# Ordering a planned kernel by due times counted back from the layers' matmuls

## The chip, the cores and the metric

One Trainium2 chip, of which the kernel uses one core. The time is that of one execution on the device, in microseconds (us); lower is better. The engines are TensorE (PE, its weight loads shown apart as PEld), VectorE (DVE), ScalarE (ACT), GpSimd (POOL) and SyncE (SP, which here issues every DMA). Each engine works through its own instructions strictly in the order in which they stand in the program, so an instruction that waits holds up all that stand behind it on its engine.

## What is computed

Eight batches of eight heads, 576 tokens, 64 values per head. Attention is computed twice: on tokens averaged in fours (144 of them), and locally, each token with the three before and the three after it. The sum of both goes through a maxout layer (three products with 512x768 weights, elementwise maximum) and an output layer of 768x512.

```python
def _attn_ref(q, k, v):
    ...
    q_d = q.reshape(B, H, Sd, factor, D).mean(axis=3)      # factor 4; k_d, v_d alike
    out_d = sm_attn(q_d, k_d, v_d)
    out_up = np.repeat(out_d, factor, axis=2)
    mask = np.abs(pos[:, None] - pos[None, :]) < factor
    scores = np.where(mask, scale * np.matmul(q, k.transpose(0, 1, 3, 2)), -1000000000.0)
    ...
    return (out_up + np.matmul(attn, v)).astype(np.float32)

def _moe_ref(x, w1, w2, w3, w_out):
    h = np.maximum(np.maximum(x @ w1, x @ w2), x @ w3)
    return (h @ w_out).astype(np.float32)
```

## The kernel before

**The work.** The 4608 tokens are nine blocks of 512 (`j` = 0 to 8; block 8 holds the last 64 tokens of every batch). Each half block of four heads has a number `n` = 2j or 2j+1. A block is first attended to, then its 512 columns go through the layers.

**The layers.** Every fp32 operand is split into a high and a low part (`hi`, `lo`) of a type that TensorE takes in one pass, and a product is three matmuls of 128x512: hi by hi, lo by hi, hi by lo. `mlp_column(j, ft, tag)` makes one of six columns of the maxout layer: three groups of 12 matmuls, each into a PSUM bank of the four called `pm`, with ACT and DVE taking the bank out (`t`, then the maximum, then `h` and its low part). `mlp_out(j)` is the output layer, four groups of 18. By the loops there are 2556 matmuls of 128x512; below they are called layer matmuls. Blocks 7 and 8 go through most of the layers together (`joint_in`), with seven products in place of eight.

**The attention.** For blocks 0 and 1 (`dense(j)`) local attention is matmuls: `band_scores` multiplies q by k in a band, `band_values` transposes the probabilities on PE (tiles `pst`, `pstb`), copies them from PSUM (`ptb`, in the buffer `y`), multiplies by v (`pxb`, bank `pq`) and copies that out (`xb`, buffer `x`). The averaged attention of the same half block (`tail_pooled`, `pooled_scores`, `band_pooled_values`, `pooled_values`) ends in `od`. `transposes(j, c)` adds both to `xs` and splits it into `xhi`, `xlo`, which the layers read. For blocks 2 to 8 (`block(j)`, `attention(n)`) local attention is elementwise: DVE multiplies (`prod`) and sums (`sums`), POOL or ACT multiplies by v (`pv`), DVE or POOL sums that (`x`).

**The weights.** 24 pieces of 512 KB (18 of the maxout layer, six of the output layer) arrive as pairs of 32-bit words and are turned into fp32 in `weight_split`: on DVE four operations on a buffer `wa` (its name in the trace is `hqk`) and a subtraction that makes `wlo` or `wo`, on ACT an absolute value and a cast.

**What sets the order.** Nothing is issued as the code runs. A `Recorder` takes each operation with the engines that could do it (`forms`), and `place()` then plays the engines by a table of prices (`price`): at each turn it takes, among the operations whose inputs are there, the one with the smallest key, puts it on the engine that ends first, and `emit()` writes the program in the order so found. Before the change the key is the time at which the operation could start, then `prio` (a number given where the operation is recorded: half blocks by 100.0 * n, matmuls 2000 lower), then the place in the code. Constants put margins into it: `LAG`, `LAG0`, `MLP`, `PE_LAG`, `BANK_LAG` (how long after its inputs an operation counts as ready) and `SPARE` (how much later than another engine DVE may be and still be chosen). PE's price is multiplied by `COLD` between `WARM` and `SLOW`.

```python
key = (t if t > now + PATIENCE[e] else now, o.prio, o.seq)
...
if e == "PE" and WARM < t < SLOW:
    c *= COLD
```

Every instruction of the trace has one line of the source, L459 (`emit`), so the rows are told apart by tiles.

Of the kernel before, what the change touches and what calls it, by code (L numbers as in the profile page):

```python
# [21 lines left out]
P = 128  # L22
# [10 lines left out]
QS = 1.0 / 128.0  # L33
QB = 1.0 / 8.0
XBUFS = 5
LAG = 678.77
LAG0 = 117.1
MLP = 601.0
PE_LAG = 2038.91
BANK_LAG = 1596.4  # L40
SEG = FAC * P
NDENSE = 2
FIRST = (0.0, 4.72, 44.91, 49.39)
LATE = (1.3, 0.0, 0.4, 9.0)
WPRIO = (20.0, 60.0, 105.0, 150.0, 160.0, 170.0, 180.0)
# [32 lines left out]

ENGINES = ("PE", "DVE", "ACT", "POOL", "SP")
DONE_NS = {"PE": 230.0, "DVE": 150.0, "ACT": 190.0, "POOL": 200.0}  # L80
SPARE = 1649.2
PATIENCE = {"PE": 0.0, "DVE": 142.18, "ACT": 0.0, "POOL": 0.0, "SP": 0.0}
LANES = 8
RING = 128
DMA_FIRST = 1300.0
DMA_LAST = 1100.0
SLOW = 82000.0
SWITCH = {("R", "P"): 120.0, ("P", "R"): 110.0, ("P", "T"): 25.0, ("T", "P"): 93.0, ("t", "P"): 90.0, ("P", "t"): 90.0, ("B", "P"): 96.0, ("M", "P"): 100.0, ("P", "M"): 20.0, ("R", "T"): 10.0, ("T", "R"): 5.0, ("R", "M"): 91.0, ("T", "M"): 93.0, ("M", "R"): 300.0, ("M", "T"): 305.0, ("M", "B"): 0.0, ("B", "M"): 96.0, ("B", "R"): 120.0, ("t", "R"): 90.0, ("R", "t"): 95.0, ("t", "M"): 90.0, ("t", "B"): 90.0, ("t", "T"): 90.0, ("T", "t"): 90.0, ("M", "t"): 100.0}
COLD = 1.65
WARM = 11000.0  # L90


def is_ap(a):
# [19 lines left out]
    return "P" if kind == "M" and elems(args[0]) in (P, 6) else kind  # L113


class Rings:
    def __init__(self):
        self.free = [0.0] * 16
# [4 lines left out]
    def issue(self, t, on_chip, outside):  # L123
        src, dst = [[list(d) for d in ap.ap] for ap in (outside, on_chip)]
        run = src.pop()[1] if src[-1][0] == 1 and len(src) > 1 else 1
        rows = int(np.prod([c for _, c in src]))
        k = max(x for x in range(1, 17) if src[0][1] % x == 0 and dst[0][1] % x == 0)
        each = rows // k
        lane = self.count % LANES
        self.count += 1  # L130
        t = max(t, self.lanes[lane])
        while True:
            left = sum(n * min(1.0, (b - max(t, a)) / (b - a)) for a, b, n in self.queue if b > t)
            if left + each <= RING or not left:
# [4 lines left out]
        work = each * (8.5 + 0.0377 * 4 * run) * (1.25 if rows > P and run > P else 1.0)  # L139
        for e in range(k):  # L140
            begin = max(self.free[e], t + DMA_FIRST)
            self.free[e] = begin + work
            if e == 0:
                self.queue.append((begin, begin + work, each))
        end = max(self.free[:k]) + DMA_LAST
        self.lanes[lane] = end
        return t, done, end


class Recorder:  # L150
# [93 lines left out]
    def price(self, eng, method, args, kw):  # L244
# [7 lines left out]
        if eng == "PE":  # L252
            rows, cols = list(args[1].ap)[0][1], elems(args[1])
            if method == "transpose":
                return (109.0 if rows == P and cols in (D, P) else 185.0 if rows > 32 else 29.0), False
            if args[1].dtype == F32R:
                return 228.5, False
            if args[1].dtype == BF16:
                return 125.0, False
            if n == SD:  # L260
                return 14.0 if cols == T32 else 66.0 if rows == T32 else 135.0 if rows == P else 209.0, False
            if cols <= D and (rows <= 16 or cols <= T32):
                return 57.0, False
            return 165.0 if n > P else 125.0, False
        if eng == "DVE":
            if method == "memset":
                return 60.0 + 0.3 * n, False
# [20 lines left out]
    def place(self):  # L288
# [45 lines left out]
        while len(out) < len(ops):  # L334
            best = None
            for e in ENGINES:
                if not queue[e]:
                    continue
                now = free[e]
                pick = None  # L340
                for o in queue[e]:
                    t = max(now, o.ready)
                    if o.cost[e][1]:
                        t = max(t, port)
                    key = (t if t > now + PATIENCE[e] else now, o.prio, o.seq)
# [19 lines left out]
            if e == "PE":  # L365
                kind = pe_kind(o)
                c += SWITCH.get((last_kind, kind), 0.0)
                last_kind = kind
            if e == "PE" and WARM < t < SLOW:
                c *= COLD  # L370
            o.eng, o.start = e, t
            if e == "SP":
                ap = next(a for a in (o.forms[e][0][1][:2]) if a.tensor.name in self.of)
# [31 lines left out]
                wake(tag)  # L405
        self.out = out
        return out

    def stuck(self, ops):
        done = set(map(id, self.out))  # L410
# [60 lines left out]
def local_global_attention_maxout_kernel(ctx: ExitStack, tc: tile.TileContext, q, k, v, qt_dense, kt_dense, qt_pool, kt_pool, qkt_tail, v_dense, v_tail, w_in, w_out, ident_d, mask_d, band_d, out):  # L471
# [51 lines left out]
    state = {"pieces": 0, "wo": []}  # L523


    def row_tokens(t, j, h, tok, n, p0=0, p1=P):
# [107 lines left out]
    def pooled_scores(n):  # L634
# [15 lines left out]
        for i in range(2):  # L650
            dve.tensor_reduce(out=nm[:, 2 * i : 2 * i + 2], in_=sps[i], axis=AX.X, op=ALU.max, negate=True)
        dve.tensor_reduce(out=nm[:, 4:5], in_=spt, axis=AX.X, op=ALU.max, negate=True)
        dve.tensor_scalar_mul(nm, nm, QS)
        for x in range(4):
            i, pr = x // 2, x % 2
            act.activation(sps[i][:, pr], sps[i][:, pr], AF.Exp, bias=nm[:, x : x + 1], scale=QS, accum_out=zd[:, x : x + 1])
# [9 lines left out]
        dve.tensor_scalar_mul(dt[:, TAIL:], spt[:, P:], rd[:, 4:5])  # L666
        rec.add(forms)
        dve.transpose(ptt[:, :T32], dt)
        for i in range(2):
# [143 lines left out]
    def band_scores(n, pr, tag):  # L813
# [7 lines left out]
        for tp in range(2):  # L821
# [13 lines left out]
            dve.tensor_scalar_mul(mx[:, :, 2 * tp : 2 * tp + 2], mx[:, :, 2 * tp : 2 * tp + 2], QB)  # L835
            for i in range(2):
                for u in range(2):
                    x = 2 * tp + u
# [293 lines left out]
    def dense(j):  # L1132
# [20 lines left out]
        if j == 0:  # L1153
            order = [load[a][0], load[b][0], load[a][1], load[b][1]] + scores[a] + sums[a] + values[a] + scores[b] + sums[b] + values[b] + [(a, pooled, 0), (b, pooled, 0)]
        else:
            order = load[a] + scores[a] + sums[a] + values[a] + load[b]
            order += [scores[b][0], sums[b][0], (a, pooled, 0), values[b][0], scores[b][1], sums[b][1], values[b][1], (b, pooled, 0)]
        for x in order:
            step(*x)

    def block(j):
        rec.spare = SPARE
# [9 lines left out]

    def weights(f, *which):
        for x in which:
            with at(40.59 + state["pieces"] * 1.14):
                f(x)

    with at(-2.0):
        load_constants()
# [69 lines left out]
```

## Time and profile before

| | |
|---|---|
| time, three runs | median 741.54 us (740.58 to 741.93) |
| the profiled execution, span from first to last instruction | 742.2 us |
| PE busy | 712.6 us, 96% of the span |
| DVE busy | 658.4 us, 89% |
| ACT busy | 422.8 us, 57% |
| POOL busy | 331.9 us, 45% |
| read from and written to HBM | 82.0 and 9.4 MB |

The profiled execution has no time of its own beside its span; the span lies 0.7 us over the median of the runs. PE's busy time counts a matmul from its start to a modelled end, and these overlap: a layer matmul counts 0.39 us and the next starts 0.23 us after it. So a PE that is 96% busy isn't 96% at work, and the clock that the profile shows as granted (PEclk, 1.00 is 2.4 GHz and 0.50 is 1.2 GHz) has to be read beside it.

### The profile page before, as it was taken

What the parts mean: (1) busy time and instruction counts of PE and PEld (TensorE: products, weight loads), DVE (VectorE), ACT (ScalarE), POOL (GpSimd) and SP (SyncE); (2) the same over time, 40 slices, a digit from 0 to 9 for tenths busy, and PEclk for the clock granted to TensorE, in tenths of its full rate; (3) what the DMA queues carried; (4) which work ended last, traced back from release to release, by engine and by line L of the source; (5) the groups of instructions that cost most, each with busy time, mean ns of one, the idle gap of its engine ahead of it and who ended that gap; (6) DMA issues with size and microseconds to landing.
All of it is one profiled execution on the core that took longest, in us unless ns stands there. A gap on an engine that the chain in (4) does not pass through costs nothing.

```text
span 742.2 us, 11812 instructions
## 1 busy us (share of the span) xinstructions
PE 712.6 (96%) x3820; PEld 566.6 (76%) x3820; DVE 658.4 (89%) x980; ACT 422.8 (57%) x1415; POOL 331.9 (45%) x545
## 2 busy tenths in 40 slices
PE   5877899999999999999999999999999999999996
PEld 3654677878788778777887787878778888888885
DVE  6999998999999998999999999999989999988520
ACT  4776767526484557557473748577395547433221
POOL 0001001038894739585573858788186336321000
PEclk9769999999999999999999999999999999999999
DMA  8954334265555535653454444633342310000012
GB/s 265 332 198 146 93 93 150 89 186 193 167 168 164 154 92 153 185 165 108 150 160 139 127 140 149 181 97 122 93 136 77 105 47 28 1 1 0 1 57 57
DMA packets 51561, 92.20 MB, mean 124 GB/s; under 512 B 5645, under 2 KB 21311, under 8 KB 51499
## 3 DMA queue, kind: packets, MB, share of 16 engines
q1 hardware_dynamic: 51498, 91.45, 39.3%
q8 instruction: 30, 0.49, 0.3%
q14 instruction: 33, 0.26, 0.1%
HBM read 81.99 MB, written 9.44 MB: 123 GB/s over the span
## 4 chain that ended last, share of the span: by engine, by line
PE 84%; DVE 7%; DMA 6%; SPq 1%; issue 1%; ACT 0%; ACTq 0%; DVEq 0%
PE pm L459 71%; PE pa L459 13%; DVE hqk L459 3%; DMA whi<-in_kt_dense_dram 2%; DMA pv<-in_kt_dense_dram 1%; DMA wo<-in_w_in_dram 1%; DMA hh<-in_w_in_dram 1%; DVE wlo_0r L459 1%; PE pq L459 1%; DMA v<-in_v_dram 1%; SPq L459 1%; DMA pv<-in_moe_w_out_dram 1%; DVE t L459 0%; DVE mxb L459 0%; DVE xlo_0r L459 0%
## 5 line engine op out<-in xcount | busy, mean ns | idle before, releaser
L459 PE MATMUL pm<-xhi_0r,whi_0r 128*128 128x512 f32 x552 | 218.3, 395 | 0.0
L459 PE MATMUL pm<-xhi_0r,wlo_0r 128*128 128x512 f32 x552 | 218.2, 395 | 0.0
L459 PE MATMUL pm<-xlo_0r,whi_0r 128*128 128x512 f32 x552 | 216.7, 397 | 0.0
L459 POOL TENSOR_TENSOR pv<-v,sums 128x256 f32<-128x256 f32 x244 | 146.7, 703 | 15.8 <-DMA v<-in_v_dram 6.0
L459 ACT ACTIVATE pv<-v,sums 128x64 f32<-128x64 f32 x536 | 141.5, 414 | 13.9 <-POOL sums L459 6.4
L459 PE MATMUL pm<-wo_0r,hh_0r 128*128 128x512 f32 x576 | 138.3, 393 | 0.5 <-DVE wo_0r L459 0.5
L459 PEld LDWEIGHTS pm<-wo_0r,hh_0r 128*128 128x128 f32 x576 | 106.7, 188 | 23.2 <-DVE wo_0r L459 0.9
L459 PEld LDWEIGHTS pm<-xlo_0r,whi_0r 128*128 128x128 f32 x552 | 103.9, 189 | 23.2 <-issue 1.1
L459 PEld LDWEIGHTS pm<-xhi_0r,wlo_0r 128*128 128x128 f32 x552 | 104.3, 189 | 22.6 <-issue 1.5
L459 PEld LDWEIGHTS pm<-xhi_0r,whi_0r 128*128 128x128 f32 x552 | 104.2, 189 | 21.8 <-issue 0.7
L459 DVE TENSOR_REDUCE sums<-prod 128x28 f32<-128x1792 f32 x56 | 112.6, 2011 | 0.5
L459 DVE TENSOR_TENSOR prod<-k,pq 128x1792 f32<-128x1792 f32 x56 | 112.1, 2002 | 0.4
L459 DVE TENSOR_REDUCE x<-pv 128x256 f32<-128x1792 f32 x44 | 88.3, 2012 | 5.0 <-ACT pv L459 3.3
L459 ACT CAST hh_0r<-pm 128x512 fp32r<-128x512 f32 x48 | 28.2, 588 | 69.7 <-DVE pm L459 69.5
L459 ACT COPY y<-pm 128x512 f32<-128x512 f32 x46 | 26.8, 589 | 53.2 <-PE pm L459 44.0
L459 POOL TENSOR_TENSOR th<-traw 128x128 f32<-128x128 f32 x25 | 11.6, 464 | 73.5 <-DVE vs L459 47.5
L459 DVE TENSOR_TENSOR t<-pm,t 128x512 f32<-128x512 f32 x46 | 31.5, 685 | 9.7 <-PE pm L459 9.7
L459 POOL TENSOR_TENSOR pv<-pv 128x768 f32<-128x768 f32 (+1 forms) x24 | 37.1, 1547 | 0.9
L459 ACT COPY pq<-q 128x256 f32<-128x256 f32 x56 | 22.3, 399 | 23.2 <-DVE prod L459 19.2
L459 ACT COPY t<-pm 128x512 f32<-128x512 f32 x44 | 25.9, 589 | 16.9 <-PE pm L459 16.4
L459 DVE TENSOR_TENSOR pm<-pm,t 128x512 f32<-128x512 f32 x46 | 31.9, 693 | 3.0 <-PE pm L459 1.9
L459 DVE TENSOR_TENSOR hh_0r<-pm,hh_0r 128x512 fp32r<-128x512 f32 x48 | 32.6, 680 | 0.9 <-ACT hh_0r L459 0.7
(321 smaller groups left out, 1096.3 us busy)
## 6 DMA issues: line engine op xcount, KB each, us to landing
k<-in_k_dram SPq DMA_DIRECT2D x55, 320.0 KB
v<-in_v_dram SPq DMA_DIRECT2D x54, 320.0 KB
out_dram<-y SPq DMA_DIRECT2D x36, 256.0 KB
q<-in_q_dram SPq DMA_DIRECT2D x56, 128.0 KB
hqk<-in_qt_pool_dram SPq DMA_DIRECT2D x24, 256.0 KB
hqk<-in_kt_pool_dram SPq DMA_DIRECT2D x24, 256.0 KB
hh<-in_w_in_dram SPq DMA_DIRECT2D x10, 512.0 KB
pv<-in_w_in_dram SPq DMA_DIRECT2D x5, 512.0 KB
```

The source lines that it names most:

```text
L459: getattr(self.engines[o.eng], method)(*map(real, args), **{k: real(x) for k, x in kw.items()})
```

## The change

The key becomes a due time. `rank()` goes through the operations from the last to the first: every layer matmul is due `STEP` before the next one, every other operation is due before those that use its result or its buffer, less its own price (`LOAD` for a DMA) and a `HOP` between engines. PE keeps its `prio`; all other engines go by due time. PE's price follows a `Clock`, which slows a matmul where the window before it held too little work. Margins, prices and the priorities of the head get new values, and DVE's operations on blocks 0 and 1 get a `spare` too. Three small multiplications that only DVE could do (`nm`, `mxb`, `dtail`) may now go to ACT. No operation is added, removed or changed in what it computes.

```diff
-LAG = 678.77
-LAG0 = 117.1
-MLP = 601.0
-PE_LAG = 2038.91
-BANK_LAG = 1596.4
+LAG = 264.42
+LAG0 = 202.26
+MLP = 1454.97
+PE_LAG = 2426.41
+BANK_LAG = 2213.91
...
-FIRST = (0.0, 4.72, 44.91, 49.39)
+FIRST = (6.48, 4.72, 31.25, 36.52)
...
+DENSE_SPARE = 291.52
+POOLED = (-3.49, 10.32, 28.62, 0.0)
...
-SPARE = 1649.2
+SPARE = 2099.53
+PATIENCE_DVE = 159.12
...
+def pe_load(o):
+    work = 0.0
+    for method, args, kw in o.forms["PE"]:
+        passes = 2.0 if method == "transpose" else 1.0 if args[1].dtype in (F32R, BF16) else 4.0
+        work += elems(args[0]) * passes * (list(args[1].ap)[0][1] / P) * (elems(args[1]) / P if method != "transpose" else 1.0)
+    return work / 2.4 / WINDOW
...
+    def at(self, t):
+        w = int((t - PHASE) // WINDOW)
+        if t < EASY:
+            return 1.0
+        return 1.0 if self.use.get(w - 1, 0.0) >= KEEP + GUARD else COLD
...
-                    key = (t if t > now + PATIENCE[e] else now, o.prio, o.seq)
+                    key = (t if t > now + (PATIENCE_DVE if e == "DVE" else 0.0) else now, o.rank, o.seq)
...
-            if e == "PE" and WARM < t < SLOW:
-                c *= COLD
+                c *= clock.at(t)
+                clock.spend(t, pe_load(o))
...
+    def rank(self):
+        for bufs, infos in self.tags.values():
+            for k, i in enumerate(infos):
+                i["by"] = 0.0
+                i["next"] = infos[k + bufs] if k + bufs < len(infos) else None
+        at = 0.0
+        for o in reversed(self.ops):
+            due = 0.0
+            for u in o.users:
+                due = min(due, u.begin - (0.0 if tuple(u.forms) == tuple(o.forms) else HOP))
+            for i in o.tiles:
+                if i["next"] is not None:
+                    due = min(due, i["next"]["by"] - HOP)
+            if "PE" in o.forms and pe_kind(o) == "R":
+                at -= STEP
+                due = min(due, at)
+            o.begin = due - (LOAD if "SP" in o.forms else min(c for c, _ in o.cost.values()))
+            for i in o.tiles:
+                i["by"] = min(i["by"], o.begin)
+            o.rank = o.prio if "PE" in o.forms else o.begin
...
-        dve.tensor_scalar_mul(nm, nm, QS)
+        scaled(nm, nm, QS)
...
-            with at(prio[n], LAG0):
+            with at(prio[n] + (POOLED[n] if f is pooled else 0.0), LAG0):
...
-            with at(40.59 + state["pieces"] * 1.14):
+            with at(WPRIO[state["groups"]]):
```

What this does to the program is seen in the order of the built instructions. The first place is **PE's queue where the band work of half block 2 (the first of block 1) stands between layer matmuls of block 0**. `pa<-prod` and `pa<-pv` are band scores, `ident,wlo` transposes of probabilities, and `pm<-xhi_0r` or `pm<-xlo_0r` layer matmuls. Before:

```order
L459 LDWEIGHTS prod_121
L459 MATMUL pa_240<-prod_121 128x268
L459 MATMUL pa_236<-pv_146 128x134
L459 MATMUL pa_240<-pv_146 128x134
L459 MATMUL pa_236<-pv_146 128x134
L459 MATMUL pa_240<-pv_146 128x134
L459 MATMUL pa_262<-ident_154,wlo_0_203 128x128 x4
L459 MATMUL pm_161<-xlo_0r,whi_0r 128x512
```

and after:

```order
L514 MATMUL pa_211<-pv_145 128x134
L514 MATMUL pm_164<-xhi_0r,wlo_0r 128x512
L514 MATMUL pm_164<-xlo_0r,whi_0r 128x512
L514 MATMUL pm_164<-xhi_0r,whi_0r 128x512
L514 MATMUL pm_164<-xhi_0r,wlo_0r 128x512
L514 MATMUL pm_164<-xlo_0r,whi_0r 128x512
L514 MATMUL pm_164<-xhi_0r,whi_0r 128x512
L514 MATMUL pm_164<-xhi_0r,wlo_0r 128x512
L514 MATMUL pm_164<-xlo_0r,whi_0r 128x512
L514 MATMUL pa_216<-ident_156,wlo_0_207 128x128 x4
```

The same first transposes of half block 2 have 35 layer matmuls ahead of them in the one queue and 60 in the other; those of the second pair have 43 and 72.

The second place is **DVE's queue at the end of half block 1's softmax** (`zb` are sums of the band's softmax, `nm` and `rd` belong to the averaged attention, `hqk` and `wlo_0r` to the weights). Before:

```order
L459 COPY y_323<-pm_164 128x512
L459 TENSOR_REDUCE nm_308<-pa_240 128x2
L459 TENSOR_TENSOR hv_231<-v_189 128x256
L459 TENSOR_SCALAR zb_287<-zb_287 128x8
L459 RECIPROCAL zb_287<-zb_287 128x8
L459 TENSOR_TENSOR hv_231<-v_195 128x256
L459 TENSOR_TENSOR wlo_0_570<-wlo_0_570,zb_287 128x536
L459 TENSOR_REDUCE nm_308<-pa_236 128x1
L459 TENSOR_SCALAR nm_308<-nm_308 128x5
```

and after:

```order
L514 TENSOR_SCALAR zb_296<-zb_296 128x8
L514 RECIPROCAL zb_296<-zb_296 128x8
L514 SCALAR_TENSOR_TENSOR hqk_341<-hh_0_329,hqk_341 128x512
L514 TENSOR_TENSOR wlo_0_543<-wlo_0_543,zb_296 128x536
L514 TENSOR_SCALAR rd_385<-pa_211 128x5
L514 TENSOR_TENSOR wlo_0r<-hqk_365,whi_0r 128x512
L514 RECIPROCAL rd_385<-rd_385 128x5
```

The copies out of PSUM (`y`) and the scaling of `nm` have left DVE, and `nm`'s maxima stand earlier, so `rd` follows at once.

The third place is **PE's queue at the averaged attention of half block 3**, the last piece that block 1 needs (`pm<-wo_0r` is the output layer of block 0, `pm<-xhi_0r` its maxout layer). Before:

```order
L459 MATMUL pa_236<-ident_154,ptail_0_123 128x128
L459 MATMUL pa_262<-ident_154,pd_421 128x128 x3
L459 MATMUL pm_159<-xlo_0r,whi_0r 128x512
L459 MATMUL pm_161<-xhi_0r,whi_0r 128x512
L459 MATMUL pm_161<-xhi_0r,wlo_0r 128x512
L459 MATMUL pm_161<-xlo_0r,whi_0r 128x512
L459 MATMUL pm_161<-xhi_0r,whi_0r 128x512
L459 MATMUL pa_240<-pt_181,vd_354 64x144 x2
```

and after:

```order
L514 MATMUL pm_161<-wo_0r,hh_0r 128x512 x9
L514 MATMUL pa_216<-ident_156,pd_398 128x128 x3
L514 MATMUL pa_229<-ident_156,pdt_404 128x128
L514 MATMUL pa_229<-ident_156,ptail_0_138 128x128
L514 MATMUL pa_216<-ident_156,pd_398 128x128
L514 MATMUL pm_161<-wo_0r,hh_0r 128x512 x6
L514 MATMUL pa_211<-pt_191,vd_408 64x144 x2
L514 MATMUL pa_216<-pt_191,vd_408 64x144 x2
```

It stood behind 172 layer matmuls and now stands behind 285, three before block 1's own begin.

## Rows read from the trace of the kernel before

**Rows 1.** The page: the span, and each engine's busy us, share and instructions.
```profile
span 742.2 us, 11812 instructions
...
PE 712.6 (96%) x3820; PEld 566.6 (76%) x3820; DVE 658.4 (89%) x980; ACT 422.8 (57%) x1415; POOL 331.9 (45%) x545
```
**Rows 2.** Windows: stretch, length, busy us (instructions) per engine, clock, DMA share, GB/s.
```profile
0.00:55.00 55.00, 39.13 (x332) 28.93 (x332) 46.36 (x149) 35.91 (x136) 1.53 (x7) 0.78 0.77 265
55.00:93.00 38.00, 30.45 (x229) 20.89 (x229) 37.48 (x89) 26.97 (x84) 2.33 (x3) 0.91 0.39 122
93.00:149.80 56.80, 56.28 (x368) 43.47 (x367) 51.85 (x115) 37.56 (x114) 4.41 (x9) 1.00 0.35 108
150.00:620.00 470.00, 470.00 (x2379) 376.99 (x2379) 447.40 (x509) 285.67 (x1015) 306.48 (x514) 1.00 0.45 138
620.00:736.00 116.00, 116.00 (x515) 96.06 (x515) 75.10 (x124) 36.10 (x68) 17.14 (x13) 1.00 0.05 16
```
**Rows 3.** Windows again, the two longest stretches at the lower clock.
```profile
19.60:29.90 10.30, 9.83 (x90) 8.07 (x90) 9.74 (x30) 7.57 (x25) 0.44 (x1) 0.51 0.98 375
40.10:53.80 13.70, 10.99 (x83) 8.83 (x83) 12.93 (x37) 11.05 (x42) 0.44 (x1) 0.51 0.47 167
```
**Rows 4.** Who PE waited for, 55 to 93 us: us, times, longest.
```profile
PE pa L459 <- ACT y L459: 1.7, 1, 1.7
PE pa L459 <- DVE hqk L459: 1.5, 1, 1.5
```
**Rows 5.** Groups of PE: xcount, busy us, mean ns; 55 to 93, then 93 to 149.8.
```profile
L459 PE MATMUL pm<-xlo_0r,whi_0r 128*128 128x512 f32 x16 | 7.5, 466 | 0.0
...
L459 PE MATMUL pm<-xlo_0r,whi_0r 128*128 128x512 f32 x56 | 22.3, 399 | 0.0
...
L459 PE MATMUL pm<-wo_0r,hh_0r 128*128 128x512 f32 x14 | 3.3, 389 | 0.0
```
**Rows 6.** The chain that ended last: start, us, what.
```profile
704.57 31.97 PE pm L459 x141
```
**Rows 7.** Single instructions of DVE, then one of PE: start, us, what.
```profile
58.31 0.68 DVE L459 TENSOR_TENSOR wlo_0r<-hqk,whi_0r 128x512 fp32r<-128x512 f32 x1
58.92 0.69 DVE L459 SCALAR_TENSOR_TENSOR hqk<-hh,hqk 128x512 uint32<-128x512 uint32 x1
...
61.99 1.28 DVE L459 TENSOR_TENSOR xlo_0r<-t,xhi_0r 128x512 fp32r<-128x512 f32 x2
...
142.11 0.68 DVE L459 TENSOR_TENSOR wlo_0r<-hqk,whi_0r 128x512 fp32r<-128x512 f32 x1
...
143.23 0.39 PE L459 MATMUL pm<-xhi_0r,whi_0r 128*128 128x512 f32 x1
```
**Rows 8.** Groups of DVE from 0 to 142.8 us: xcount, busy us, mean ns.
```profile
L459 DVE TENSOR_TENSOR hv<-v 128x256 f32<-128x256 f32 x8 | 3.3, 407 | 2.1 <-DMA v<-in_v_dram 2.1
L459 DVE TENSOR_SCALAR mxb<-mxb 128x4 f32<-128x4 f32 x16 | 2.9, 181 | 0.2
L459 DVE COPY y<-pm 128x512 f32<-128x512 f32 x4 | 2.7, 686 | 0.3 <-PE pm L459 0.3
...
L459 DVE TENSOR_TENSOR th<-traw 128x128 f32<-128x128 f32 x3 | 0.8, 282 | 0.0
```
**Rows 9.** Groups of POOL and ACT; the first row to 142.8 us, the rest whole span.
```profile
L459 POOL TENSOR_TENSOR th<-traw 128x128 f32<-128x128 f32 x6 | 2.8, 468 | 71.0 <-DVE vs L459 47.5 <-DVE mxb L459 17.9 <-DMA traw<-in_qkt_tail_dram 3.4
...
L459 POOL TENSOR_TENSOR th<-pt 128x128 f32<-128x128 f32 x1 | 1.3, 1303 | 21.5 <-ACT xhi_0r L459 21.5
...
L459 POOL TENSOR_TENSOR x<-whi_0r,wlo_0r 128x512 f32<-128x512 f32 x10 | 14.2, 1440 | 24.9 <-DVE x L459 23.0 <-DVE pa L459 2.0
...
L459 ACT COPY pt<-pa 128x512 f32<-128x512 f32 x15 | 8.9, 592 | 0.6 <-PE pa L459 0.6
```
**Rows 10.** Timeline: block 2's last sum on DVE, its transposes on PE.
```profile
223.43 2.02 DVE L459 TENSOR_REDUCE x<-pv 128x256 f32<-128x1792 f32 x1 [0.91 <-POOL pv L459]
...
238.85 0.60 PE L459 MATMUL pa<-ident,x 128*128 128x128 f32 x4
```

More of the change, by code (lines that the diff above doesn't have):

```diff
@@ L35 @@
 XBUFS = 5
[L36 to L40 removed]
+LAG = 264.42
[3 more added lines that the diff above has]
+BANK_LAG = 2213.91
 SEG = FAC * P
 NDENSE = 2
[L43 removed]
+FIRST = (6.48, 4.72, 31.25, 36.52)
 LATE = (1.3, 0.0, 0.4, 9.0)
[L45 removed]
+WPRIO = (40.59, 44.01, 47.43, 50.85, 54.27, 55.41, 56.55, 57.69, 58.83, 62.25, 65.67, 66.81)
+DENSE_SPARE = 291.52
+POOLED = (-3.49, 10.32, 28.62, 0.0)
 SETS = (5, 4, 3, 2, 5, 4, 5, 5)
@@ L84 @@
 RING = 128
-DMA_FIRST = 1300.0
+DMA_FIRST = 1600.0
 DMA_LAST = 1100.0
-SLOW = 82000.0
+WINDOW = 3413.3
+PHASE = 2200.0
+KEEP = 0.352
+EASY = 0.0
+GUARD = 0.03
+HOP = 214.54
+STEP = 311.26
+LOAD = 5701.23
 SWITCH = {("R", "P"): 120.0, ("P", "R"): 110.0, ("P", "T"): 25.0, ("T", "P"): 93.0, ("t", "P"): 90.0, ("P", "t"): 90.0, ("B", "P"): 96.0, ("M", "P"): 100.0, ("P", "M"): 20.0, ("R", "T"): 10.0, ("T", "R"): 5.0, ("R", "M"): 91.0, ("T", "M"): 93.0, ("M", "R"): 300.0, ("M", "T"): 305.0, ("M", "B"): 0.0, ("B", "M"): 96.0, ("B", "R"): 120.0, ("t", "R"): 90.0, ("R", "t"): 95.0, ("t", "M"): 90.0, ("t", "B"): 90.0, ("t", "T"): 90.0, ("T", "t"): 90.0, ("M", "t"): 100.0}
-COLD = 1.65
-WARM = 11000.0
+COLD = 1.9
 def is_ap(a):
@@ L113, in pe_kind, with __init__, spend @@
     return "P" if kind == "M" and elems(args[0]) in (P, 6) else kind
+def pe_load(o):
[4 more added lines that the diff above has]
+    return work / 2.4 / WINDOW
+class Clock:
+    def __init__(self):
+        self.use, self.fast = {}, {}
+    def at(self, t):
[3 more added lines that the diff above has]
+        return 1.0 if self.use.get(w - 1, 0.0) >= KEEP + GUARD else COLD
+    def spend(self, t, load):
+        w = int((t - PHASE) // WINDOW)
+        self.use[w] = self.use.get(w, 0.0) + load
 class Rings:
@@ L138, in issue @@
         self.queue = [x for x in self.queue if x[1] > t]
-        work = each * (8.5 + 0.0377 * 4 * run) * (1.25 if rows > P and run > P else 1.0)
+        work = each * (8.5 + 0.0408 * 4 * run) * (1.25 if rows > P and run > P else 1.0)
         for e in range(k):
@@ L263, in price @@
                 return 57.0, False
-            return 165.0 if n > P else 125.0, False
+            return 118.0 if n > P else 109.0, False
         if eng == "DVE":
@@ L302, in place @@
                 i["todo"], i["at"], i["end"] = len(i["ops"]), None, 0.0
+        self.rank()
         freed = {t: [(0.0, i) for i in range(b)] for t, (b, _) in self.tags.items()}
@@ L308, in place @@
         rings = Rings()
+        clock = Clock()
         queue = {e: [] for e in ENGINES}
@@ L522, in local_global_attention_maxout_kernel @@
     whi, wlo = [None] * NFT, [None] * NFT
-    state = {"pieces": 0, "wo": []}
+    state = {"pieces": 0, "groups": 0, "wo": []}
     def row_tokens(t, j, h, tok, n, p0=0, p1=P):
@@ L665, in pooled_scores @@
         forms = {"DVE": [("tensor_scalar_mul", (pdt, spt[:, :P], rd[:, 4:5]), {})], "ACT": [("mul", (pdt, spt[:, :P], rd[:, 4:5]), {})]}
-        dve.tensor_scalar_mul(dt[:, TAIL:], spt[:, P:], rd[:, 4:5])
+        rec.add({"DVE": [("tensor_scalar_mul", (dt[:, TAIL:], spt[:, P:], rd[:, 4:5]), {})], "ACT": [("mul", (dt[:, TAIL:], spt[:, P:], rd[:, 4:5]), {})]})
         rec.add(forms)
@@ L834, in band_scores @@
                 dve.tensor_reduce(out=mx[:, i, 2 * tp : 2 * tp + 2], in_=sps[i], axis=AX.X, op=ALU.max, negate=True)
-            dve.tensor_scalar_mul(mx[:, :, 2 * tp : 2 * tp + 2], mx[:, :, 2 * tp : 2 * tp + 2], QB)
+            scaled(mx[:, :, 2 * tp : 2 * tp + 2], mx[:, :, 2 * tp : 2 * tp + 2], QB)
             for i in range(2):
@@ L1157, in dense @@
             order += [scores[b][0], sums[b][0], (a, pooled, 0), values[b][0], scores[b][1], sums[b][1], values[b][1], (b, pooled, 0)]
+        rec.spare = DENSE_SPARE
         for x in order:
             step(*x)
+        rec.spare = 0.0
     def block(j):
@@ L1174, in weights @@
         for x in which:
-            with at(40.59 + state["pieces"] * 1.14):
+            with at(WPRIO[state["groups"]]):
                 f(x)
+            state["groups"] += 1
     with at(-2.0):
```

## Prediction

> **What bounds the kernel now.** Read the page first [rows 1]: PE is busy for 96% and DVE for 89%, so either may set the end, and an average doesn't say where. The chain of waits does: its last link is a run of 141 matmuls on PE with no other engine in it [rows 6], which is 31.97/141 = 0.227 us for one layer matmul. Then cut the span into stretches [rows 2]. From 150 to 736 us PE is busy for 586 of 586 us at a granted clock of 1.00, the upper level of 2.4 GHz; from 93 to 149.8 us it lacks 0.52 us. Behind 93 us nothing can be gained by making anything else faster: PE works through its queue, and the last layer matmul ends at 736.5, followed by a copy and a store.
>
> Ahead of 93 us PE loses time, and busy time understates how much, because matmuls overlap and run longer at the lower clock. So I count work. From 93 to 149.8 us there are 368 matmul records, 180 of them of the layers (four groups, the first 56 and the last 14 [rows 5]). These take 180 x 0.227 = 40.9 us of the 56.28 busy, and the other 188 share 15.4 us, 0.082 us each. At these prices the stretches ahead hold:
> - 0 to 55 us: 332 records, four of the layers: 0.9 + 328 x 0.082 = 27.8 us of work, 27.2 us lost.
> - 55 to 93 us: 229 records, 47 of the layers (three groups, the first 16 [rows 5]): 10.7 + 182 x 0.082 = 25.6 us, 12.4 us lost.
>
> The kernel is thus some 702 us of PE's work and 39.6 us of loss, all in the head. The first part of the loss is the start: transfers fill 0.77 of the DMA time there, and the attention to blocks 0 and 1 has to exist before the layers can have input. In the second part DVE is the one that never rests, 37.48 of 38 us [rows 2]. PE's own waits there are for copies out of PSUM (`y`, 1.7 us) and for weights in the making (`hqk`, 1.5 us) [rows 4], and its clock is 0.91 on average. All of block 0's layer work (over 50 us) could fill these gaps, if its input `xlo` and the weights were there. The last pair of `xlo` tiles of block 0 comes from DVE at 61.99 to 63.27 us, the last maxout weight at 142.79 [rows 7]. So the question is how much sooner DVE gets there, and whether PE's queue is ordered to use it.
>
> **The change, part by part.** *DVE ahead of block 0's `xlo`.* By the order, 27 operations that stood ahead of it on DVE now stand elsewhere: five copies out of PSUM at 0.69 go to ACT (3.4 us; the `y` copy in [rows 8]); six scalings of `mxb` at 0.18 and two of `nm` at the same go to ACT (1.4); one `pdt` (0.3) likewise; 12 additions go to POOL: four of `hv` at 0.41, four of `th` at 0.28 [rows 8], and four more of these sizes (0.2 to 0.7), 4.1 in all. One more `mxb` scaling (0.2) only stands later. That is 9.4 us. Three operations stand ahead that didn't: two on weights (0.69 and 0.42) and a maximum of `mxb` (0.43), 1.5 us. Net some 7.7 us of durations and 24 instructions. Durations overlap: one that takes 0.68 from 58.31 ends 0.07 after the next starts [rows 7]. With 0.08 for each of 24, the queue is 5.8 us shorter, and `xlo` is complete at 63.3 - 5.7 = 57.6 us.
>
> *DVE ahead of the last maxout weight.* By the same count 23.6 us of durations and some 65 instructions go, among them all 13 `mxb` scalings that move (2.4 us), nine copies (6.2) and 18 additions (5.8); start to start some 19 us. Each weight piece thus comes at least 5.7 us sooner, the later ones up to 19 us. PE takes that piece up at 143.23 [rows 7]. After the change it gets there 11.6 us sooner by what it regains, and has 1.8 us less work ahead of it in its queue: 129.8, with the piece ready at 142.8 - 19 = 124. The same sum leaves the other pieces of the last two columns some 6 us or more and the earlier columns over 10. So weights don't become late; if this cover fails, the price is in rival B.
>
> *PE's queue.* Moving DVE sooner pays only if PE has layer matmuls where the attention isn't ready. It has: 60 instead of 35 stand ahead of half block 2's first transposes and 72 instead of 43 ahead of the second pair, 25 x 0.227 = 5.7 us of filler. That answers the waits of [rows 4]: copies that made PE wait go to ACT, and what is still late is now behind more matmuls. In place of a stretch of 38 us with 12.4 us lost, a stretch to 57.6 us loses at the old rate, 12.4 x 2.6/38 = 0.8, and then nothing. **Gain 11.6 us.**
>
> *The other end of that.* The attention of block 1 is only put off: the averaged attention of half block 3 had 172 layer matmuls ahead of it and now has 285, three short of those of block 1 itself. From it run a copy on ACT (0.59), an addition (0.69 on DVE, 1.44 on POOL [rows 9]), a cast on ACT (0.59) and a subtraction (0.68, or 1.44 on POOL): 2.6 to 4.1 us end to end. Three layer matmuls hide 0.7 us, other PE work that stands there up to 2 more. I charge 1 us, with bounds of 0 (more matmuls of block 0's output layer hide it) and 4 (nothing does).
>
> *ACT.* 74 instructions more: ten copies at 0.59 [rows 9] and 46 small ones of about 0.2, at most 15 us over the head, and the pieces of six `pv` products of the later blocks. From 55 to 93 us ACT is busy for 27 of 38 us [rows 2], so 11 us are free and this hides; if not, a copy that waits holds a PSUM bank and PE waits as for `y` (1.7 us a time). *POOL* has 2.33 us of work in 38 and room for 21 additions. *Blocks 2 to 8* are ordered anew as well, DVE's work per block changing by a few us. The nearest hand-over, to block 2, had 238.85 - 225.45 = 13.4 us between DVE's last sum and its transposes [rows 10]: nothing. *The first 55 us*: DVE is freed there too, but transfers hold 0.77 of DMA time, and the changed order of loads can go either way; 0, with bounds of -4 and +4.
>
> Sum: 742.2 - 11.6 + 1 + 0 = 731.6 us for an execution like the profiled one. That one lies 0.7 us over the median of the runs, so **731.0 us**.
>
> A row speaks against a part of this: an addition of `th` took 0.468 us on POOL in the mean, but one of them, beside the DVE that never rests, 1.303 us [rows 9], against 0.28 on DVE [rows 8]. The Trainium skill ("SBUF — State Buffer", "Who interferes with whom") says why it may be worse: a DVE instruction with two inputs in SBUF and a POOL instruction that reads SBUF shut each other out for its whole length. The trace agrees as to POOL's time; that DVE pays too no row shows. By that rule 21 additions at about 0.7 us would hold DVE for 14.6 us, `xlo` would come hardly sooner, and the gain would be 3.5 to 7 us in place of 10.6.
>
> **The rivals.** *A, the forecast:* the stretch fills; 727 to 735.
> *B, half of it:* in-order PE waits where a piece is put too late or a weight column isn't ready, or DVE is held up by POOL's additions. For it: the hand-overs are ordered by a table of prices, and POOL's 1.303 us against 0.468 shows that a price may not hold. Against: PE lacks 0.52 us in the 56.8 behind 93 us, under the same kind of table. A wait of 4 us in place of 1, and 2 to 3 us of weights, leave some 5 us of gain: 736.
> *C, the first stretch shrinks too:* DVE is 46.36 of 55 us busy and carries the clock's low half with it: in the two stretches at 0.51, PE has 9.83 and 10.99 us busy [rows 3], at the lower level, 1.2 GHz. If freed DVE time ends one of them 3 to 6 us sooner: 725.
> *D, slower:* the hand-over to block 1. PE has nothing else to do between the 285th and 288th matmul; if the four steps behind it queue behind DVE's long sums (2.02 us each [rows 10]) instead of running straight, PE stands for 3 to 6 us, and the clock falls to the lower level as it did for 10.3 and 13.7 us in the head [rows 3]. At half clock 10.3 us holds half the work: 5.1 us lost, on top of the wait. Twice (block 1, and again at block 2, whose attention is then as late) that is 16 to 22 us: 742.2 - 11.6 + 18 - 0.7 = 748. [...] The Trainium skill ("TensorE: Matmul & The Clock Gate", "Why this matters for your kernels") has the same: gaps of idle time between bursts put the clock back to its half; the two stretches in the trace are such a case.
> *E, it doesn't do what it says:* prices of the order don't match the chip, waits move to other pieces, and DVE, still full, feeds PE no sooner: 741.
>
> **How the numbers follow.** A 0.60, B 0.17, C 0.13, D 0.06, E 0.04. The likeliest is A, 731.0. B and its bounds reach to 738 (a gain of 3.5 us is 738), C to 725; D, E and the outer tails are left out, under 2 in 10. About 0.2% (1.5 us) is what a measurement of this kernel can tell from no change: faster 0.90 (A, B, C), same 0.04 (E), slower 0.06 (D).
>
> **What would show it.** DVE's last `xlo` of block 0 near 57.6 us and the last maxout weight near 124; in a stretch from 58 to 93 us PE near 35 us busy at 1.00 with some 50 more layer matmuls than before; no wait over 2 us ahead of block 1's first matmul; the last layer matmul near 726. It is wrong if `xlo` comes at 62 or later (the queue got no shorter on the chip), if `hqk` or `wlo` head PE's waits (weights late), if a wait for `od` or `xlo` of block 1 is followed by a lower clock (D), or if the loss ahead of 55 us differs from 27 us by more than 4.

## The result, and the profile after

The changed kernel takes 734.06 us (median of 7 runs, 733.21 to 740.04), the kernel before 741.93 us in the same series: a ratio of 0.990, 95% interval 0.9877 to 0.9924, or 7.9 us. Forecast were 731.0 us, and a gain of 10.6, of which three quarters were measured.

The profiled execution of after spans 731.9 us, where the sum of the prediction gave 731.6. In every run of either kernel the time lies some 1.75 us over the span (733.65 us for this one). By that, the span of 742.2 us in [rows 1] belongs to an execution of some 744 us, longer than any of the seven timed ones of before (740.58 to 742.34). The kernel before, profiled once more (`before_again` below), has a span of 739.5 us and a time of 741.24, 0.7 under its median, as that of after lies 0.4 under its own; so after is held against that profile from here on, and like for like the gain is 7.6 us of span.

The page of after, as in [rows 1]:

```profile
span 731.9 us, 11900 instructions
...
PE 709.9 (97%) x3820; PEld 565.8 (77%) x3820; DVE 618.6 (85%) x889; ACT 435.1 (59%) x1489; POOL 391.0 (53%) x602
```

DVE has 40 us of work less, ACT 12 and POOL 59 more. The same windows as in [rows 2], first of before (its second profile), then of after (stretch, length, busy us and instructions of PE, PEld, DVE, ACT and POOL, granted clock, DMA share, GB/s):

```profile
0.00:55.00 55.00, 43.07 (x351) 31.95 (x355) 48.92 (x155) 37.82 (x141) 1.53 (x7) 0.91 0.82 279
55.00:93.00 38.00, 30.64 (x223) 21.35 (x220) 37.41 (x88) 26.63 (x87) 2.35 (x3) 0.91 0.37 115
149.80:300.00 150.20, 150.20 (x747) 120.19 (x745) 145.02 (x158) 86.47 (x304) 104.40 (x177) 1.00 0.53 162
```
```profile
0.00:55.00 55.00, 40.03 (x353) 30.39 (x354) 45.35 (x134) 41.05 (x159) 10.57 (x20) 0.88 0.82 277
55.00:93.00 38.00, 37.81 (x279) 28.07 (x278) 36.55 (x78) 30.22 (x101) 6.38 (x10) 1.00 0.41 132
93.00:149.80 56.80, 56.75 (x355) 44.16 (x355) 51.10 (x93) 35.59 (x103) 11.47 (x22) 1.00 0.43 139
149.80:300.00 150.20, 149.33 (x759) 117.99 (x759) 146.97 (x161) 101.09 (x373) 128.64 (x201) 1.00 0.53 163
```

From 55 to 93 us PE is full, at 1.00, and does 100 layer matmuls there in place of 53. DVE is about as full there as before (36.55 us for 37.41), and nothing is gained ahead of 55 us. From 150 to 300 us PE lacks 0.87 us, one wait. With each kind of PE's instruction at its median pace behind 95 us (the kinds that only the head has, at that of their fastest fifth), the time that PE lost can be estimated (us):

| stretch | before | after |
|---|---|---|
| 0 to 55 us | 26.9 | 27.1 |
| 55 to 93 us | 13.0 | 2.2 |
| 93 to 200 us | 1.8 | 2.0 |
| 200 to 300 us | -0.3 | 2.4 |
| 300 us to the last layer matmul | 0.4 | 0.6 |

By this count 10.8 us are gained in the stretch that the prediction named, and 3.3 of them lost again in the others, 2.7 of that between 200 and 300 us. Counted with mean paces in place of median ones, the second row is 13.1 and 1.9 and the fourth -0.9 and 3.1: the gain of some 11 us stands, the other rows hold to about 1.3 us. The milestones of DVE, and the end of the chain of waits, of after:

```profile
57.67 1.29 DVE L514 TENSOR_TENSOR xlo_0r<-t,xhi_0r 128x512 fp32r<-128x512 f32 x2
...
128.32 0.68 DVE L514 TENSOR_TENSOR wlo_0r<-hqk,whi_0r 128x512 fp32r<-128x512 f32 x1
...
694.00 31.97 PE pm L514 x141
```

Block 0's last `xlo` ends at 58.96 us (forecast 57.6), the last maxout weight at 129.0 (forecast 124), the last layer matmul at 725.97 (forecast 726).

### The profile page after: what moved, and what is told of

Its sections match the earlier page's. It is cut to its first block, busy times and chain, and to the rows that moved or that the text cites. A ratio compares the mean times of both kernels' runs of the same rounds, so it can differ in the third digit from the quotient of the medians.

```text
span 731.9 us, 11900 instructions
## 1 busy us (share of the span) xinstructions
PE 709.9 (97%) x3820; PEld 565.8 (77%) x3820; DVE 618.6 (85%) x889; ACT 435.1 (59%) x1489; POOL 391.0 (53%) x602
## 4 chain that ended last, share of the span: by engine, by line
PE 86%; DVE 7%; issue 1%; ACT 1%; DMA 0%; DVEq 0%; SPq 0%; ACTq 0%
PE pm L514 72%; PE pa L514 14%; DVE hqk L514 3%; PE pq L514 1%; DVE t L514 1%; DVE wlo_0r L514 1%; DVE mxb L514 1%; DVE xlo_0r L514 1%; DMA traw<-in_v_tail_dram 0%; ACT wlo L514 0%; DVE prod L514 0%; DVE q L514 0%; DVE hh_0r L514 0%; DVE pm L514 0%; DVE qkT L514 0%
## 5 line engine op out<-in xcount | busy, mean ns | idle before, releaser
L514 ACT ACTIVATE pv<-v,sums 128x64 f32<-128x64 f32 x560 | 145.8, 415 | 18.2 <-POOL sums L514 8.0
L514 POOL TENSOR_TENSOR pv<-v,sums 128x256 f32<-128x256 f32 x238 | 142.0, 699 | 3.7 <-DMA v<-in_v_dram 2.1
L514 POOL TENSOR_TENSOR pv<-pv 128x768 f32<-128x768 f32 (+1 forms) x50 | 77.5, 1550 | 2.3
L514 DVE TENSOR_REDUCE x<-pv 128x256 f32<-128x1792 f32 x31 | 62.3, 2011 | 4.6 <-ACT pv L514 2.5
L514 ACT COPY y<-pm 128x512 f32<-128x512 f32 x50 | 29.3, 594 | 46.0 <-PE pm L514 40.1
L514 POOL TENSOR_TENSOR x<-whi_0r,wlo_0r 128x512 f32<-128x512 f32 x10 | 14.1, 1417 | 47.7 <-DVE x L514 30.4
L514 POOL TENSOR_TENSOR hv<-v 128x128 f32<-128x128 f32 (+1 forms) x52 | 25.3, 497 | 25.4 <-DMA v<-in_v_dram 25.2
```

The costliest lines, as they stand in the source:

```text
L514: getattr(self.engines[o.eng], method)(*map(real, args), **{k: real(x) for k, x in kw.items()})
```

## The experiments

Times are given against the kernel before in the same series; after is 7.9 us under it in its own. The median of before lies between 741.93 and 742.34 us in the four series, so a difference from after carries up to 0.4 us of that. Seven of the kernels change nothing but the engine of some operations: the planned order stays, and then

```diff
         out = self.place()
+        to = {s: e for e, seqs in MOVED.items() for s in seqs}
+        for o in out:
+            o.eng = to.get(o.seq, o.eng)
```

with `MOVED` a list of operations. (In the three that are built from before, the three small multiplications also get a second form, for ACT.) In the head 57 operations change their engine by the change: 21 additions (DVE to POOL) and 36 copies, scalings and normalizations (nearly all DVE to ACT).

**before_again**: no edit.

> The kernel before, unchanged, profiled once more, since the profiled pair differs by 10.3 us (742.2 to 731.9) and the medians by 7.9 us (741.93 to 734.06). If the profiled execution of before was a long one of its kind, this one has a span near 740 us, with less than the 13.4 us that PE lost from 55 to 93 us in the first profile, and the medians are right: some 7.9 us gained. If the span is 742 again, the difference lies in what is timed around the span.

Measured: 741.91 us, span 739.5. The first profile was a long execution; block 0's `xlo`, at 63.3 us there, is complete at 60.74 here. So of the 4.3 us by which `xlo` seems to come sooner, 2.5 were that execution's.

**order_only**: after's order, all 57 operations on before's engines.

> The changed kernel's order on every engine, with all 57 operations of the head on the engines that the kernel before had them on: the new order alone. Theory: xlo ends at 59.0 + 7.2 - 1.2 = 65, later than before (63.3), and 5 to 6 us of the 7.9 are lost: 2 us under before. Rival (the order, and with it the matmuls that fill PE's gaps, is what brings the gain): 6 us or more under before.

Measured: 740.32 us, 2.0 under before by the medians, 0.7 by the means (ratio 0.999, 0.9971 to 1.0008: no difference that can be told). The theory's number came out, but the profile shows two things that cancel (windows of this kernel, columns as above):

```profile
0.00:55.00 55.00, 38.72 (x302) 28.61 (x304) 46.29 (x149) 36.30 (x138) 1.68 (x7) 0.68 0.78 267
55.00:93.00 38.00, 35.35 (x286) 26.36 (x287) 37.31 (x88) 25.99 (x82) 2.90 (x3) 0.97 0.38 118
```

With the new order alone, and `xlo` later than before (63.75 us), PE is fuller from 55 to 93 us than before (35.35 for 30.64), and it pays for that ahead of it (302 instructions to 55 us in place of 351; part of that is the clock of this execution, 0.68 for 0.91, whose time was 742.03 us, 1.7 over the median; seven of the 12 runs lie from 739.42 to 740.35 us, five from 742.03 to 746.73) and behind it. Counted with mean paces, as above, PE loses 8.3 us less than before from 55 to 93 us, and 4.1 us more ahead of that, 2.0 more from 93 to 200 and 3.9 more from 200 to 300 us. Only the head's engines are those of before: over the whole span DVE is 629.6 us busy here and 659.4 in before, so what changed its engine in the later blocks counts as part of the order.

**engines_only**: before's order, the 57 operations on after's engines.

> The order of the kernel before on every engine, with the 57 operations of the head on the engines that the change puts them on: the moves alone. By durations DVE reaches block 0's last xlo 7 us sooner than before, at 57 us with the stretching by POOL. Theory (both parts are needed, since PE's queue has only 35 and 43 layer matmuls ahead of half block 2's transposes in place of 60 and 72): half of the gain, 3 to 5 us under before. Rival (DVE's time is all): 7 to 8 us under before. Rival (order is all): within 1 us of before.

Measured: 745.14 us, 3.2 *slower* than before (ratio 1.0049, 1.0034 to 1.0064). All three expectations fell. DVE has 7 us less to do ahead of `xlo` by durations, 4.8 us less as it ran, and yet is later with it, at 62.57. Windows up to that point for this kernel, and who DVE waited for there (us, times, longest):

```profile
0.00:62.57 62.57, 44.49 (x371) 31.26 (x372) 49.81 (x138) 44.96 (x165) 9.36 (x21) 0.83 0.79 266
```
```profile
DVE mxb L470 <- PE pm L470: 2.9, 1, 2.9
DVE q L470 <- DMA whi<-in_qt_dense_dram: 2.4, 2, 2.0
DVE wlo_0r L470 <- ACT whi_0r L470: 2.0, 1, 2.0
DVE hqk L470 <- ACT hqk L470: 1.5, 2, 1.2
DVE zb L470 <- ACT wlo L470: 1.1, 2, 0.7
```

DVE is idle for 12.8 of 62.57 us; in before it was idle for 6.1 of 60.74. What was taken off its queue came back as waits; the three for ACT that are shown are 4.6 us.

**acts_only** and **adds_only**: before's order, with the 36 moves between DVE and ACT alone, and with the 21 additions alone.

> The order of the kernel before, with only the 36 moves between DVE and ACT of the head (copies and small scalings to ACT). All 57 moves in that order were 3.2 us slower than before. Theory now: in the old order each copy and scaling stands on ACT behind exponentials and weight parts that were placed there for another division of labour, so DVE and PE wait for ACT instead (waits for ACT's wlo, hqk and whi): 2 to 4 us slower than before. Rival (it was the additions on POOL that cost): within 1 us of before, or faster.

> The order of the kernel before, with only the 21 additions of the head moved from DVE to POOL. Theory: as in the changed kernel's order, where putting them back on DVE cost 0.4 us, DVE gains what it doesn't do itself and pays it back where POOL's instruction holds it up: within 1 us of before. Rival: POOL's result comes later (0.5 to 0.8 us in place of 0.3 to 0.4) and those that wait for it are late: 2 us slower or more.

Measured: 744.59 us, 2.6 slower (1.0024 to 1.0048), and 742.65 us, 0.7 slower (1.0004 to 1.0026). The copies and scalings on ACT are what costs in the old order; the additions on POOL bring nothing there.

**adds_back**: after's order, the 21 additions on DVE again.

> The changed kernel's order as it is, with the 21 additions of the head that moved from DVE to POOL put back on DVE at the same place. Theory: DVE's time ahead of block 0's last xlo sets the gain; 12 additions of 4.1 us come back (3.2 us start to start) and the 1.2 us go by which POOL's additions stretch DVE's own work, so xlo ends at 61 in place of 59.0 us and the time is 2 us longer than the changed kernel's, 6 under before. Rival (an addition on POOL costs DVE as much as doing it itself): xlo at 59 and no difference. Rival (DVE isn't what sets the gain): xlo later, time unchanged.

Measured: 734.74 us, 7.6 under before, 0.3 from after; `xlo` ends at 58.5 us in place of 59.0. The first rival holds: these additions on POOL save DVE nothing. Part of the reason is in the time line of after (start, us, instruction):

```profile
23.14 1.14 POOL L514 TENSOR_TENSOR hv<-v 128x256 f32<-128x256 f32 x1 [6.43 <-DMA v<-in_v_dram]
23.60 0.95 DVE L514 TENSOR_SCALAR hqk<-hqk 128x512 f32<-128x512 f32 x1
24.23 0.64 POOL L514 TENSOR_TENSOR th<-k 128x128 f32<-128x128 f32 x1
...
24.55 0.60 DVE L514 TENSOR_TENSOR hv<-v 128x256 f32<-128x256 f32 x1
```

and of the same place in adds_back:

```profile
23.29 0.42 DVE L522 TENSOR_SCALAR hqk<-hqk 128x512 f32<-128x512 f32 x1
...
24.13 0.38 DVE L522 TENSOR_TENSOR hv<-v 128x256 f32<-128x256 f32 x1
...
24.86 0.28 DVE L522 TENSOR_TENSOR th<-k 128x128 f32<-128x128 f32 x1
```

Beside POOL's `hv`, DVE's `hqk` takes 0.95 us in place of 0.42; alone, DVE does that addition in 0.38. The other part is waiting. Up to the end of `xlo` the window of adds_back is

```profile
0.00:58.48 58.48, 43.20 (x375) 32.47 (x376) 50.66 (x154) 43.64 (x165) 3.75 (x9) 0.88 0.84 284
```

so with 13 instructions more DVE is busy for only 1.3 us more than in after (49.32 us), and it is idle for 7.8 us in place of 9.6.

**act_back** and **copies_back**: after's order, with the 36 moves put back, and with the ten large copies alone put back.

> The changed kernel's order, with the 36 operations of the head that moved between DVE and ACT (copies out of PSUM, the small scalings) put back. Theory: 4.1 us come back on DVE ahead of xlo, which ends at 63, and the time is 4 us longer than the changed kernel's, 4 under before. Rival (the order of the work is what brings the gain): xlo later, but time within 1 us of the changed kernel's.

> The changed kernel's order, with only the ten large copies out of PSUM put back from ACT to DVE; the small scalings stay on ACT. All 36 moves put back cost 4.2 us. Theory: DVE's time decides, and the five copies ahead of block 0's last xlo are 3.0 of the 4.1 us there: 3 us longer than the changed kernel, 4 to 5 under before. Rival (the scalings decide, since each stands between a maximum and an exponential that PE's next transposes wait for): 1 us or less longer.

Measured: 738.58 us, 3.8 under before, so 4.1 longer than after; and 737.20 us, 4.7 under before, so 3.2 longer than after. Both times are as the theories had them: in the new order what DVE does itself counts, the copies hold three quarters of it, and the rival on the scalings falls. The way isn't the theories'. `xlo` ends at 61.3 us in act_back, where 63 was expected, and at 60.0 in copies_back, where the three quarters called for 62: 2.3 and 1.0 us later than in after, for 4.1 and 3.2 us of time. The rest is lost in other places, among them PE's wait for the probabilities that DVE normalizes. From 45 to 93 us, in after, act_back and copies_back:

```profile
PE pm L514 <- DVE wlo L514: 0.9, 1, 0.9
...
PE pm L523 <- DVE wlo L523: 1.8, 1, 1.8
...
PE pm L522 <- DVE wlo L522: 1.9, 1, 1.9
```

**old_clock**: planned anew with the old factor on PE's price:

```diff
-                c *= clock.at(t)
+                c *= 1.65 if 11000.0 < t < 82000.0 else 1.0
```

> The changed kernel planned anew with the fixed factor of 1.65 on PE's price between 11 and 82 us in place of the one that follows recent use; due times and the rest as changed. The order that results has less filler on PE (43 and 49 layer matmuls ahead of half block 2's transposes in place of 60 and 72), and DVE reaches xlo 2.4 us sooner by durations. Theory: the two cancel, 0 to 2 us longer than the changed kernel. Rival (filler decides): 3 us or more longer. Rival (xlo decides): 2 us shorter.

Measured: 746.36 us, 4.4 slower than before and 12.3 longer than after. `xlo` ends at 59.8, 0.8 later than in after where 2.4 sooner was expected, and the gaps are back (window of this kernel, and PE's longest waits from 45 to 93 us):

```profile
55.00:93.00 38.00, 29.73 (x200) 20.69 (x201) 32.65 (x65) 25.46 (x82) 6.95 (x9) 0.82 0.32 109
```
```profile
PE pa L514 <- ACT wlo L514: 4.7, 4, 2.2
PE pq L514 <- ACT wlo L514: 2.3, 2, 1.7
PE pa L514 <- ACT pt L514: 1.2, 1, 1.2
```

With 43 and 49 layer matmuls ahead of half block 2's transposes in place of 60 and 72, PE stands at the softmax (`wlo` holds its probabilities). The rival "filler decides" holds, and more strongly than it said. It's an order planned anew, so all queues differ, not the filler alone.

**band_sooner**: the band attention of half blocks 2 and 3 earlier in PE's queue, all other queues as in after. The order is put together again with

```diff
-        out = self.place()
+        out = self.refill(self.place())
```

where `refill()` keeps each engine's sequence but gives every piece of band attention the number of layer matmuls ahead of it that before had, as far as the inputs allow.

> The changed kernel with one thing undone in PE's queue: the band attention of half blocks 2 and 3 stands where the kernel before had it, as far as the other queues allow (36 layer matmuls ahead of half block 2's first transposes in place of 60, 48 ahead of the second pair in place of 72, 120 in place of 131 ahead of half block 3's). Engines and all other queues are the changed kernel's. Theory: 24 matmuls, 5.4 us of filler, are missing where PE waits for the softmax; the scores come sooner too, which gives back some of it: 2 to 4 us longer than the changed kernel. Rival (the filler isn't needed once DVE is quick): within 0.5 us of it.

Measured: 782.27 us, 40.3 slower than before, 48 longer than after. Far off what was expected. The waits of PE from 45 to 93 us, and of DVE from 55 to 150 us, in this kernel:

```profile
PE pa L590 <- ACT wlo L590: 10.8, 5, 4.2
...
DVE t L590 <- PE pm L590: 18.3, 4, 8.9
DVE pm L590 <- PE pm L590: 9.0, 3, 3.8
DVE zb L590 <- ACT wlo L590: 7.8, 2, 4.4
```

DVE's queue still takes the layers' products out (`t`) ahead of the softmax. PE now wants the softmax before it makes those products. By these waits, each waits for the other in turn. The run shows that these queues fit only as a set; it doesn't price 24 matmuls of filler.

**by_prio**: planned anew with the old key, all else as changed:

```diff
-            o.rank = o.prio if "PE" in o.forms else o.begin
+            o.rank = o.prio
```

> The changed kernel planned anew with the key of the kernel before (priorities in place of due times for all engines); everything else, the clock in PE's price, the margins and the two extra engine choices included, as changed. By durations, DVE reaches block 0's last xlo 3.5 us later than in the changed kernel and the last maxout weight 4 us later; PE's filler is the same (61 and 75 ahead of half block 2's transposes). Theory: the time follows xlo: 3 to 4 us longer than the changed kernel. Rival (due times don't matter, the moves off DVE do): within 1 us of it.

Measured: 761.05 us, 19.1 slower than before. `xlo` ends at 74.2 us, not at 62.5 as the durations had it, and PE waits 7.3 us for weights behind 93 us. The due times are needed under these constants; whether other constants would do as well with the old key wasn't tried.

**handover_late**: after, with PE's last transposes and averaged attention of half block 3 at 288 layer matmuls (`refill()` again), and the eight additions and subtractions that lead to block 1's `xlo` on POOL (six instructions more there than in after).

> The changed kernel with the hand-over to block 1 made tighter on purpose: the last transposes and the averaged attention of half block 3 stand directly ahead of block 1's first layer matmul (288 layer matmuls ahead of them in place of 279 and 285), and all sums that follow are on POOL at 1.3 to 1.75 us each. Theory: PE waits in pieces for 3 to 5 us between 148 and 162 us, the granted clock stays at 1.00 and the time is 3 to 5 us longer than the changed kernel's. Rival (D of the prediction: a standstill sends the clock to its lower level): a stretch at 0.50 behind the wait, and 8 us longer or more.

Measured: 734.86 us, 7.1 under before, 0.8 longer than after. Between 148 and 162 us PE stands once, for 0.68 us, at 1.00:

```profile
151.01 0.71 PE L595 MATMUL pa<-pt,vd 128*64 128x144 f32 x8 [0.68 <-ACT pt L595]
```

Behind it PE goes on with scores of block 2 (`qkT`) and with products of the part of block 1 that is ready. Neither expectation held: the hand-over has more cover than both gave it.

## Why the prediction was right, and where it wasn't

**The place was right.** The stretch from 55 to 93 us was to lose 0.8 us in place of 12.4; by the prediction's own count after loses 38 - 100 x 0.227 - 179 x 0.082 = 0.6 us there. The clock at 1.00, 34.81 us busy of 35 from 58 us on and 47 layer matmuls more (some 50 forecast) are as it said. [rows 4] has no counterpart: no wait of PE of over 0.2 us in that stretch.

**The reason was half right.** The sum let the gain follow from DVE's queue ahead of `xlo`, 5.8 us shorter, with PE's filler only as a condition. The four corners show the weights (the engines are those of the 57 operations of the head, the order all else):

| | before's engines | after's engines |
|---|---|---|
| before's order | 0 | 3.2 slower |
| after's order | 2.0 faster | 7.9 faster |

Neither part brings a gain that can be told from none; rival E's doubt was true for each of them alone. In the old order the moves make it slower, in the new one they bring 5.9 us, 3.2 of them by the ten copies. The step that failed is "the queue is 5.8 us shorter, and `xlo` is complete at 63.3 - 5.7 = 57.6 us". Like for like `xlo` comes 1.8 us sooner, from 60.74 to 58.96. Windows from 0 to that point, of before and of after:

```profile
0.00:60.74 60.74, 46.48 (x371) 33.83 (x372) 54.62 (x166) 41.80 (x150) 2.54 (x8) 0.91 0.80 274
```
```profile
0.00:58.96 58.96, 44.00 (x375) 33.22 (x376) 49.32 (x141) 43.42 (x165) 11.24 (x22) 0.88 0.82 278
```

DVE's busy time falls by 5.3 us, its idle time rises from 6.1 to 9.6. The count of durations was good (its parts add up to 7.9 us, not 7.7); that DVE would run through without standing was not, and [rows 2] had shown it idle for 8.6 of the first 55 us. From 55 us to the end of `xlo` DVE doesn't rest; ahead of that, where most of the removed work stood, it waits for transfers and for ACT.

With `xlo` only 1.8 us sooner, the stretch from 55 to 93 us still gave back nearly what was forecast, so a sum with a wrong step came out in part by luck. What filled the stretch goes with PE's order and not with the date of `xlo`:

| kernel | layer matmuls ahead of half block 2's two pairs of transposes | `xlo` complete, us | layer matmuls from 55 to 93 us |
|---|---|---|---|
| before | 35, 43 | 60.7 | 53 |
| engines_only | 35, 43 | 62.6 | 48 |
| old_clock | 43, 49 | 59.8 | 47 |
| order_only | 60, 72 | 63.8 | 81 |
| after | 60, 72 | 59.0 | 100 |

order_only has `xlo` 3.0 us later than before and does 28 layer matmuls more in the stretch; old_clock has it 0.9 us sooner and does six fewer. With the moves the new order does 100 in place of 81. These kernels differ in whole queues, so that the filler alone does it isn't shown.

**The rule that was weighed holds.** The prediction counted 12 additions, 4.1 us, as taken off DVE. adds_back shows that they are worth nothing. DVE does pay: its instructions ahead of `xlo` are stretched by some 1.8 us in sum against the median of their kind (0.6 in before). By the Trainium skill ("SBUF — State Buffer", "Who interferes with whom") DVE and POOL contend only for the pair of ports that they share, and that pair is an exclusive lock. The trace agrees roughly: DVE's `hqk` above, held to the end of POOL's `hv`, would end at 24.28 + 0.42 = 24.70 us, and ends at 24.55. It takes one tile as input (it clamps weights), and isn't one of the instructions with two inputs that the prediction named. But that `xlo` would then hardly come sooner wasn't a reason for a smaller gain: the price was paid on DVE, and the gain came from PE's queue.

**The hand-over** was charged 1 us at block 1, and block 2 nothing, by 13.4 us of slack [rows 10]. It's the other way round: at block 1 PE doesn't wait, at block 2 it does (227.38 us, for the bank that DVE empties):

```profile
227.38 0.63 PE L514 MATMUL pa<-ident,x 128*128 128x128 f32 x4 [0.87 <-DVE xlo_0r L514]
```

This 0.87 us is a third or less of what is lost between 200 and 300 us; the rest isn't a wait that the profile shows, and its cause stays open. Slack read from before doesn't hold where the change orders the place anew.

**From the span to the median.** The prediction took 0.7 us off since the span of its profile lay 0.7 over the median of three runs. With the time 1.75 over the span, that execution was some 2.4 us longer than a typical one, and 2.4 - 1.75 is the same 0.7: the step holds, but the sum of 731.6 us was one for an execution as long as that. The profile of after is a typical one, so that its span of 731.9 us meets 731.6 is luck. Like for like 7.6 of 10.6 us were gained; by the table above, 0.8 us of the rest is in the stretch from 55 to 93 us (10.8 for 11.6), and 2.3 in the others (3.3 lost where 1 was charged).

**Rival D** wasn't met: no standstill at block 1 or 2 reaches 1 us. **C** wasn't either: 27.1 us are lost ahead of 55 us, as before.

## What to carry to other kernels

Where in-order engines are planned together, take an order and its division of labour as one thing: moving work off the busiest engine without planning anew made this kernel slower, and planning anew without the moves brought no gain that can be told from none. Before a shorter queue is counted as time, look at that engine's idle time in the very stretch in which the work stood; and hold a profile's span against timed runs by the constant between them, since one profiled execution can be 2.7 us from the next.

## What the runs showed of the hardware

POOL's addition held up DVE, not only DVE the addition: DVE's TENSOR_SCALAR on `hqk` took 0.95 us beside it in place of 0.42, and even the one on `zb` with 8 values a partition 0.49 in place of 0.17 (13.29 us in after).

The granted clock can fall to its lower level after a standstill of PE, and the 10 us that rival D took from [rows 3] do occur behind the head. In by_prio PE stands from 138.7 us for 2.1 us and soon after runs, busy throughout, at 0.50 for 10.2 us; in band_sooner it stands from 98.1 to 102.6 us and then runs at 0.50 for 6.6 us. The length of the standstill doesn't settle it: one of 1.6 us in band_sooner, at 155.5, is followed by 1.00, and one of 1.5 us in before, at 58.5, by 3.4 us at 0.50. In the order of this text:

```profile
138.70:140.80 2.10, 0.07 (x1) 0.07 (x1) 2.03 (x6) 1.15 (x5) 0.19 (x1) 1.00 0.52 199
...
141.30:151.50 10.20, 10.20 (x71) 7.83 (x71) 9.02 (x17) 7.57 (x20) 2.19 (x4) 0.50 0.40 138
```

```profile
98.10:102.60 4.50, 0.08 (x3) 0.05 (x2) 4.28 (x8) 1.47 (x3) 0.00 (x0) 0.99 0.00 0
102.60:109.20 6.60, 6.60 (x48) 5.54 (x49) 5.84 (x14) 3.97 (x13) 0.00 (x0) 0.50 0.54 159
...
155.50:157.10 1.60, 0.07 (x2) 0.05 (x1) 0.36 (x1) 1.55 (x4) 0.00 (x0) 1.00 0.00 0
157.10:162.00 4.90, 4.90 (x30) 3.33 (x31) 4.20 (x9) 3.75 (x9) 0.00 (x0) 1.00 0.26 79
```
```profile
58.50:60.00 1.50, 0.04 (x2) 0.00 (x0) 1.50 (x4) 0.97 (x5) 0.00 (x0) 1.00 0.72 254
...
60.40:63.80 3.40, 3.40 (x14) 2.06 (x13) 3.40 (x7) 2.19 (x4) 1.50 (x2) 0.50 0.63 185
```
